# Spectral mixing and a gated feed-forward block on one core: the first batch's loads, buffers and weight roundings rearranged

## The chip, the cores and the metric

One core of a Trainium2 chip. The metric is device time in microseconds (us), the median of several runs. Lower is better. The kernel before took 3157.78 us (median of three runs, 3153.94 to 3158.0).

## The reference, cut to what matters

```python
batch, seq, dim = (8, 3008, 256)            # x: float32
X = np.fft.rfft(x, axis=1)                  # 1505 frequencies
Y = X * (filt_r + 1j * filt_i)[None]        # a learned filter, float32
y = np.fft.irfft(Y, n=3008, axis=1).astype(np.float32)
x = y.reshape(8 * 3008, 256)                # 24064 tokens
g = x @ w_gate                              # 256 -> 1536; the three weights are float64
silu = g * (1.0 / (1.0 + np.exp(-g)))
out = (silu * (x @ w_val) @ w_out).astype(np.float32)
```

The kernel does the transform as matrix products: a first step over 47 rows ("pa"), a middle step per pair of frequencies ("pb", product with the filter, "pc") and an inverse step ("pd"). Between these the data goes through DRAM (d1 and d2) to be regrouped. Then come blocks of the feed-forward part ("hidden blocks", tiles wA, wE, wF with g or v) and its output products (tiles ending in _o), done as seven products for eight. While the hidden blocks of one batch run on TensorE, the transform of the next batch is slipped in between. Only the first batch has nothing to hide behind.

The float64 weights arrive as pairs of 32-bit words and are rounded to float32 by bit operations: 18 "roundings", each a chain over VectorE, ScalarE and GpSimd.

## The kernel before

The parts that the change and the argument touch (`...` marks cuts):

```python
def round_weights(j):
    load_weights(j + 2)                     # two raw buffers, two loads ahead
    ...
    v.tensor_scalar(out=man, in0=high, scalar1=0xFFFFF, scalar2=None, op0=ALU.bitwise_and)
    nc.scalar.activation(out=w, in_=man, func=AF.Copy, scale=2.0 ** -20, bias=1.0)
    v.tensor_scalar(out=pw, in0=high, scalar1=20, scalar2=0x7FF, ...)
    v.tensor_scalar(out=pw, in0=pw, scalar1=-896.0, scalar2=0.0, op0=ALU.add, op1=ALU.max)
    ...                                     # three more operations on VectorE
    nc.gpsimd.tensor_tensor(out=w, in0=w, in1=pw.bitcast(FP32), op=ALU.mult)
    ...                                     # three copies on ScalarE, four sums on GpSimd

def load_tables(self, parts=3):             # first batch: 3 x (1 table + 4 filter parts)
    for i in range(parts):
        nc.sync.dma_start(out=tb[:, ts(i, n)], in_=de_dram[:, ts(i, n)])
        for rows, view in filter_parts():   # 32 partitions each, every second one reversed
            nc.sync.dma_start(out=f[rows, ts(i, n), :], in_=view(n * i, n))
    ...

def stage1(self, u):
    ...
    nc.tensor.matmul(out=ps[0:NK], lhsT=wf_t, rhs=self.x.pop(u), ...)    # pa, 94x96
    nc.scalar.copy(out=t1, in_=ps[0:NK])
    nc.gpsimd.dma_start(out=self.d1_rows[:, ts(u, NV), :], in_=t1)

def stage2a(self, u):
    ...
    ps = fps.tile(...)                      # pb shares two PSUM banks with pa, pc, pd
    ...                                     # two matmuls, four products on VectorE
    add(nc.gpsimd, pt, pt, qt)

def stage2b(self, u):
    ps = fps.tile(...)                      # pc
    ...
    nc.scalar.copy(out=g, in_=ps)
    for p in range(2):
        nc.gpsimd.dma_start(out=self.d2[...], in_=g[64 * p:64 * p + 64])

# the first batch
spec.load_x(0); load_weights(0); load_weights(1); spec.load_tables()
for u in range(N_ONE): spec.stage1(u)
for _ in range(2): round_weights(todo.pop(0))
for u in range(N_TWO + 1):                  # pc follows pb by one step
    if u < N_TWO: spec.stage2a(u)
    if u: spec.stage2b(u - 1)
...
if b == 0 and i == 0:                       # the filter, copied inside DRAM for later batches
    for rows, view in filter_parts():
        nc.scalar.dma_start(out=f_dram[rows], in_=view(0, NS))
```

The order in which each engine runs its instructions is set by a scheduler when the kernel is built. It moves the roundings and the filter copy to where the engine concerned looks free.

## Time and profile before

| Stretch of the kernel before | us from the start |
|---|---|
| first load of d1 (row "t<-d" of SyncE's timeline) | 61.95 |
| first pd | 143.93 |
| first hidden block | 153.92 |
| end of the second output product | 287.07 |
| end of the span | 3160.8 |

The stretches are read from timelines. TensorE's gives each group of matmuls with start, duration, array size and, in square brackets, the idle time before it and what released it.

### The profile page before, as it was taken

What the parts mean: (1) busy time and instruction counts of PE and PEld (TensorE: products, weight loads), DVE (VectorE), ACT (ScalarE), POOL (GpSimd) and SP (SyncE); (2) the same over time, 40 slices, a digit from 0 to 9 for tenths busy, and PEclk for the clock granted to TensorE, in tenths of its full rate; (3) what the DMA queues carried; (4) which work ended last, traced back from release to release, by engine and by line L of the source; (5) the groups of instructions that cost most, each with busy time, mean ns of one, the idle gap of its engine ahead of it and who ended that gap; (6) DMA issues with size and microseconds to landing.
All of it is one profiled execution on the core that took longest, in us unless ns stands there. A gap on an engine that the chain in (4) does not pass through costs nothing.

```text
span 3160.8 us, 40740 instructions
## 1 busy us (share of the span) xinstructions
PE 3059.3 (97%) x15488; PEld 2241.2 (71%) x15488; DVE 1474.2 (47%) x2348; ACT 1150.4 (36%) x2122; POOL 1418.7 (45%) x1662
## 2 busy tenths in 40 slices
PE   4689999999999999999999999999999999999998
PEld 1456777777776777777777677777777677777776
DVE  2664554345544445335543355434554345544443
ACT  1244333333334333333334433333333433333332
POOL 2664454345443445344444445434544345533343
PEclk9589999999999999999999999999999999999999
DMA  8522222213222222122222222221321212210000
GB/s 253 140 87 66 80 67 66 60 54 93 67 57 70 61 73 81 56 62 71 73 64 60 66 77 71 60 67 54 87 74 50 72 55 77 64 30 21 21 8 13
DMA packets 112691, 215.61 MB, mean 68 GB/s; under 512 B 19672, under 2 KB 53464, under 8 KB 111480
## 3 DMA queue, kind: packets, MB, share of 16 engines
q1 hardware_dynamic: 84208, 134.86, 14.9%
q0 software_dynamic: 26624, 75.01, 8.3%
q10 hardware_dynamic: 1664, 3.15, 0.3%
q8 instruction: 122, 2.00, 0.3%
q14 instruction: 73, 0.60, 0.1%
HBM read 137.96 MB, written 78.12 MB: 68 GB/s over the span
## 4 chain that ended last, share of the span: by engine, by line
PE 78%; POOL 7%; DVE 5%; issue 2%; ACT 2%; POOLq 0%; DVEq 0%
PE wA_v L396 15%; PE wA_g L396 15%; PE wA_o L460 7%; PE wE_v L396 7%; PE wE_g L396 7%; PE wE_o L460 7%; PE wF_o L460 4%; PE wF_g L396 4%; PE pd L354 3%; PE wF_v L396 3%; POOL o L160 3%; PE pa L305 3%; POOL h L163 3%; PE pc L336 2%; PE pb L317 2%
## 5 line engine op out<-in xcount | busy, mean ns | idle before, releaser
L396 PE MATMUL wA_v<-y,wv_t 128*128 128x376 f32 x1536 | 614.7, 482 | 10.0 <-ACT u_v L405 9.2
L396 PE MATMUL wA_g<-y,wg_t 128*128 128x376 f32 x1536 | 614.9, 482 | 5.7 <-ACT s L416 3.3
L163 POOL TENSOR_TENSOR h<-h 128x376 f32<-128x376 f32 x576 | 566.7, 984 | 28.8
L160 POOL TENSOR_TENSOR h<-h 128x376 f32<-128x376 f32 x192 | 188.1, 980 | 709.1 <-PE wE_v L396 407.6
L405 ACT COPY u_g<-wA_g 128x376 f32<-128x376 f32 x576 | 269.8, 468 | 588.5 <-PE wA_g L396 585.9
L396 PEld LDWEIGHTS wA_v<-y,wv_t 128*128 128x128 f32 x1536 | 290.1, 190 | 206.6 <-DVE h L418 15.8
L460 PEld LDWEIGHTS wA_o<-wo_t,h 128*128 128x128 f32 x3456 | 406.9, 192 | 16.6 <-issue 0.6
L460 PE MATMUL wA_o<-wo_t,h 128*128 128x128 f32 x3456 | 417.9, 275 | 0.0
L396 PEld LDWEIGHTS wA_g<-y,wg_t 128*128 128x128 f32 x1536 | 281.9, 191 | 173.1 <-issue 28.7
L423 ACT ACTIVATE s<-s 128x1128 f32<-128x1128 f32 x192 | 219.5, 1143 | 375.7 <-DVE s L160 375.7
L425 DVE TENSOR_TENSOR h<-s,h 128x1128 f32<-128x1128 f32 x192 | 258.2, 1345 | 125.6 <-ACT s L423 125.5
L396 PE MATMUL wE_g<-y,wg_t 128*128 128x376 f32 x768 | 308.1, 483 | 0.0
L396 PE MATMUL wE_v<-y,wv_t 128*128 128x376 f32 x768 | 307.6, 482 | 0.2 <-DVE h L160 0.2
L405 ACT COPY u_v<-wA_v 128x376 f32<-128x376 f32 x576 | 272.6, 473 | 69.6 <-PE wA_v L396 65.9
L160 DVE TENSOR_TENSOR s<-u_g,wE_g 128x376 f32<-128x376 f32 x384 | 209.1, 544 | 177.7 <-ACT u_g L405 176.1
L160 DVE TENSOR_TENSOR s<-u_g,wF_g 128x376 f32<-128x376 f32 x192 | 104.5, 544 | 399.2 <-PE wF_g L396 377.8
L460 PE MATMUL wE_o<-wo_t,h 128*128 128x128 f32 x2304 | 281.6, 276 | 7.6 <-DVE o L160 7.6
L460 PE MATMUL wF_o<-wo_t,h 128*128 128x128 f32 x2304 | 278.3, 275 | 0.0
L460 PEld LDWEIGHTS wE_o<-wo_t,h 128*128 128x128 f32 x2304 | 267.5, 192 | 13.7 <-DVE o L160 13.7
L460 PEld LDWEIGHTS wF_o<-wo_t,h 128*128 128x128 f32 x2304 | 267.6, 192 | 0.0
L160 DVE TENSOR_TENSOR h<-u_v,wE_v 128x376 f32<-128x376 f32 x384 | 209.2, 545 | 27.9 <-ACT u_v L405 6.0
L160 POOL TENSOR_TENSOR p<-p,q 128x512 f32<-128x512 f32 x96 | 121.9, 1270 | 212.0 <-DVE q L327 207.3
(66 smaller groups left out, 3285.5 us busy)
## 6 DMA issues: line engine op xcount, KB each, us to landing
d<-t POOLq DMA_DIRECT2D x128, 192.0 KB, 2.4
t<-d SPq DMA_DIRECT2D x192, 128.0 KB, 2.9
d<-g POOLq DMA_DIRECT2D x192, 128.0 KB, 2.6
t<-d SPq DMA_DIRECT2D x64, 384.0 KB, 3.9
tb<-de_tbl SPq DMA_DIRECT2D x84, 256.0 KB, 3.8
f<-filt SPq DMA_DIRECT2D x84, 256.0 KB, 2.7
x<-in_x_dram SPq DMA_DIRECT2D x112, 160.0 KB, 2.3
out_dram<-o POOLq DMA_DIRECT2D x128, 128.0 KB, 2.0
```

The lines of the kernel that those rows point to most:

```text
L160: eng.tensor_tensor(out=dst, in0=a, in1=b, op=ALU.add)
L163: eng.tensor_tensor(out=dst, in0=a, in1=b, op=ALU.subtract)
L305: nc.tensor.matmul(out=ps[0:NK], lhsT=wf_t, rhs=self.x.pop(u), start=True, stop=True)
L317: nc.tensor.matmul(out=ps[:, i, :], lhsT=self.tb[u][:, i, 0, :], rhs=t2[:, i, :], start=True, stop=True)
L336: nc.tensor.matmul(out=ps[:, i, :], lhsT=tb[:, i, 1, :], rhs=pt[:, i, :], start=True, stop=True)
L354: nc.tensor.matmul(out=psv[:, n, :], lhsT=self.t4[k, i][:, n, ts(cb, 128)], rhs=wi_t, start=True, stop=True)
L396: nc.tensor.matmul(out=bk[z][kind], lhsT=wt[z][:, j, LEFT[p], :], rhs=y[:, RIGHT[p], :], start=start, stop=True, skip_group_check=True)
L405: nc.scalar.copy(out=u[(1, 6, 7).index(p)], in_=bk[z]["A"])
L423: nc.scalar.activation(out=s[:, 0:3], in_=s[:, 0:3], func=AF.Silu)
L425: nc.vector.tensor_tensor(out=h[:, 0:3], in0=s[:, 0:3], in1=h[:, 0:3], op=ALU.mult)
L460: nc.tensor.matmul(out=bk[kind][:, t, :], lhsT=hs[i][:, HID[p], t0:t0 + 128], rhs=wo_t[:, JB * q + i, RIGHT[p], :], start=start and t == 0 ...
```

## The change

The intent: make the first batch shorter. The pb of the first batch get six PSUM banks of their own, and pc follows by three steps instead of one. The table loads go to ScalarE's queue and half of the d2 writes to ScalarE. Roundings are held in program order ("pin") so that they cannot slide into the first batch. One of their operations goes to ScalarE, and three copies vanish because GpSimd writes straight to the destination. The filter is no longer copied inside DRAM. The diff, cut to its core:

```diff
-    f_dram = fdpool.tile([128, NS, C], FP32, name="filt")
+        pin = tc.keep_in_program_order
-        v.tensor_scalar(out=man, ...)
-        nc.scalar.activation(out=w, in_=man, func=AF.Copy, ...)
-        v.tensor_scalar(out=pw, in0=pw, scalar1=-896.0, scalar2=0.0, op0=ALU.add, op1=ALU.max)
+        pin(v.tensor_scalar(out=man, ...))
+        pin(nc.scalar.activation(out=w, in_=man, func=AF.Copy, ...))
+        pin(nc.scalar.activation(out=pw, in_=pw, func=AF.Relu, bias=off_t))
-        nc.gpsimd.tensor_tensor(out=w, in0=w, in1=pw.bitcast(FP32), op=ALU.mult)
+        pin(e.tensor_tensor(out=dst[:, 0:4, :]..., in0=w, in1=pw.bitcast(FP32), op=ALU.mult))
-            for p, a in ((1, w[:, 0, 0]), (2, w[:, 0, 1]), (4, w[:, 1, 1])):
-                nc.scalar.copy(out=dst[:, LEFT[p]], in_=a)
...                                     # load_x: into the space of weights not yet there
-                    nc.sync.dma_start(out=self.f[u], in_=f_dram[:, ss])
+                    for rows, view in filter_parts():
+                        self.load(out=self.f[u][rows], in_=view(NV * u, NV))
-                nc.sync.dma_start(out=tb[:, ts(i, n)], in_=de_dram[:, ts(i, n)])
+                nc.scalar.dma_start(out=tb[:, ts(i, n)], in_=de_dram[:, ts(i, n)])
                 for rows, view in filter_parts():
-                    nc.sync.dma_start(out=f[rows, ts(i, n), :], in_=view(n * i, n))
+                    nc.scalar.dma_start(out=f[rows, ts(i, n), :], in_=view(n * i, n))
-            nc.gpsimd.dma_start(out=self.d1_rows[:, ts(u, NV), :], in_=t1)
+            queue = nc.scalar if self.b == 1 else nc.gpsimd
+            queue.dma_start(out=self.d1_rows[:, ts(u, NV), :], in_=t1)
+                ps = bank("AEF"[u % 3], f"b_{u}").rearrange("p (i c) -> p i c", i=NV)
-                nc.gpsimd.dma_start(out=self.d2[...], in_=g[64 * p:64 * p + 64])
+                queue = nc.scalar if self.b == 0 and p else nc.gpsimd
+                queue.dma_start(out=self.d2[...], in_=g[64 * p:64 * p + 64])
-        spec.load_x(0)
+        for i in range(4):
+            spec.load_x(i)
+        spec.load_tables()
         load_weights(0)
         load_weights(1)
-        spec.load_tables()
-        for u in range(N_TWO + 1):
+        lag = 3
+        for u in range(N_TWO + lag):
-            if b == 0 and i == 0:
-                for rows, view in filter_parts():
-                    nc.scalar.dma_start(out=f_dram[rows], in_=view(0, NS))
```

More of the change, by code (lines that the diff above doesn't have):

```diff
@@ L62 @@
 N_TWO = NS // NV
-LEFT = {1: 0, 2: 1, 4: 2, 5: 3, 6: 4, 7: 5, 3: 6}
+LEFT = {1: 0, 2: 1, 7: 2, 4: 3, 5: 4, 6: 5, 3: 6}
 RIGHT = {1: 0, 2: 1, 3: 2, 4: 3, 5: 4, 6: 5, 7: 6}
+WO = {1: 0, 7: 1, 2: 2, 3: 3, 5: 4, 6: 5, 4: 6}
 HID = {1: 0, 6: 1, 4: 2, 2: 3, 5: 4, 7: 5, 3: 6}
@@ L134 @@
     dpool = pool("dram", 2, DRAM)
-    fdpool = pool("fdram", 1, DRAM)
     fps = pool("fps", 2, PSUM)
@@ L143 @@
     wo_t = cpool.tile([128, NJ, 7, 128], FP32)
-    f_dram = fdpool.tile([128, NS, C], FP32, name="filt")
+    off_t = cpool.tile([128, 1], FP32)
+    nc.vector.memset(off_t, -896.0)
     def filter_parts():
@@ L205, in round_weights @@
         flat2 = "p a b f two -> p (a b f) two"
-        v.tensor_scalar(out=man, in0=high, scalar1=0xFFFFF, scalar2=None, op0=ALU.bitwise_and)
-        nc.scalar.activation(out=w, in_=man, func=AF.Copy, scale=2.0 ** -20, bias=1.0)
-        v.tensor_scalar(out=pw, in0=high, scalar1=20, scalar2=0x7FF,
-                        op0=ALU.logical_shift_right, op1=ALU.bitwise_and)
-        v.tensor_scalar(out=pw, in0=pw, scalar1=-896.0, scalar2=0.0, op0=ALU.add, op1=ALU.max)
+        pin = tc.keep_in_program_order
+        pin(v.tensor_scalar(out=man, in0=high, scalar1=0xFFFFF, scalar2=None,
+                            op0=ALU.bitwise_and))
+        pin(nc.scalar.activation(out=w, in_=man, func=AF.Copy, scale=2.0 ** -20, bias=1.0))
+        pin(v.tensor_scalar(out=pw, in0=high, scalar1=20, scalar2=0x7FF,
+                            op0=ALU.logical_shift_right, op1=ALU.bitwise_and))
+        pin(nc.scalar.activation(out=pw, in_=pw, func=AF.Relu, bias=off_t))
         v.tensor_scalar(out=pw, in0=pw, scalar1=255.0, scalar2=2.0 ** 23,
@@ L218, in round_weights, with bank @@
                                op0=ALU.mult, op1=ALU.add)
-        nc.gpsimd.tensor_tensor(out=w, in0=w, in1=pw.bitcast(FP32), op=ALU.mult)
         e = nc.gpsimd
+        pin(e.tensor_tensor(out=dst[:, 0:4, :].rearrange("p (a b) f -> p a b f", b=2), in0=w,
+                            in1=pw.bitcast(FP32), op=ALU.mult))
         if left:
-            for p, a in ((1, w[:, 0, 0]), (2, w[:, 0, 1]), (4, w[:, 1, 1])):
-                nc.scalar.copy(out=dst[:, LEFT[p]], in_=a)
-            add(e, dst[:, LEFT[5]], w[:, 1, 0], w[:, 1, 1])
-            sub(e, dst[:, LEFT[6]], dst[:, LEFT[5]], w[:, 0, 0])
-            sub(e, dst[:, LEFT[7]], w[:, 0, 0], w[:, 1, 0])
-            sub(e, dst[:, LEFT[3]], w[:, 0, 1], dst[:, LEFT[6]])
-        else:
-            for p, a in ((1, w[:, 0, 0]), (2, w[:, 1, 0]), (3, w[:, 1, 1])):
-                nc.scalar.copy(out=dst[:, RIGHT[p]], in_=a)
-            sub(e, dst[:, RIGHT[5]], w[:, 0, 1], w[:, 0, 0])
-            sub(e, dst[:, RIGHT[6]], w[:, 1, 1], dst[:, RIGHT[5]])
-            sub(e, dst[:, RIGHT[7]], w[:, 1, 1], w[:, 0, 1])
-            sub(e, dst[:, RIGHT[4]], w[:, 1, 0], dst[:, RIGHT[6]])
+            a11, a12, a21, a22, s1, s2, s4 = [dst[:, i] for i in range(7)]
+            add(e, s1, a21, a22)
+            sub(e, s2, s1, a11)
+            sub(e, a21, a11, a21)
+            sub(e, s4, a12, s2)
+        else:
+            b11, b12, b21, b22, t1, t2, t4 = [dst[:, i] for i in range(7)]
+            sub(e, t1, b12, b11)
+            sub(e, t2, b22, t1)
+            sub(e, b12, b22, b12)
+            sub(e, t4, b21, t2)
+    def bank(kind, name):
+        return wps.tile([128, 512], FP32, name=f"w{kind}_{name}", tag=kind)
     class Spectral:
@@ L247, in __init__, with load @@
             self.x, self.t2, self.f, self.tb, self.p, self.t4, self.y = {}, {}, {}, {}, {}, {}, {}
+        def load(self, **kw):
+            ins = nc.sync.dma_start(**kw)
+            if self.b == 1:
+                tc.keep_in_program_order(ins)
         def load_x(self, u):
             if self.b == 0:
-                if u == 0:
-                    rows = x[0].rearrange("(r n) c -> r n c", n=32)
-                    for i in range(4):
-                        xt = spool0.tile([NR, 8, C], FP32, name=f"x0_{i}", tag="x", bufs=2)
-                        for r in (slice(0, 80), slice(80, NR)):
-                            nc.sync.dma_start(out=xt[r], in_=rows[r, ts(i, 8), :])
-                        for j in range(8 // NV):
-                            self.x[8 // NV * i + j] = xt[:, ts(j, NV), :]
+                rows = x[0].rearrange("(r n) c -> r n c", n=32)
+                for a, n in ((0, NV), (NV, 8 - NV)) if u == 0 else ((0, 8),):
+                    for r in (slice(0, 80), slice(80, NR)):
+                        nc.sync.dma_start(out=x0[u][r, a:a + n, :],
+                                          in_=rows[r, 8 * u + a:8 * u + a + n, :])
+                for j in range(8 // NV):
+                    self.x[8 // NV * u + j] = x0[u][:, ts(j, NV), :]
             elif u < N_ONE:
@@ L263, in load_x @@
                 for r in (slice(0, 80), slice(80, NR)):
-                    nc.sync.dma_start(out=self.x[u][r], in_=rows[r, ts(u, NV), :])
+                    self.load(out=self.x[u][r], in_=rows[r, ts(u, NV), :])
         def load_two(self, u):
@@ L268, in load_two @@
                 b = self.b
-                ss = ts(u, NV)
                 if b:
                     self.tb[u] = tbpool.tile([128, NV, 2, 128], FP32, name=f"tb_{b}_{u}", tag="tb")
-                    nc.sync.dma_start(out=self.tb[u], in_=de_dram[:, ss])
+                    self.load(out=self.tb[u], in_=de_dram[:, ts(u, NV)])
                     self.f[u] = fpool.tile([128, NV, C], FP32, name=f"f_{b}_{u}", tag="f")
-                    nc.sync.dma_start(out=self.f[u], in_=f_dram[:, ss])
-                self.t2[u] = t2pool.tile([128, NV, C], FP32, name=f"t2_{b}_{u}", tag="t2")
+                    for rows, view in filter_parts():
+                        self.load(out=self.f[u][rows], in_=view(NV * u, NV))
+                p2 = spool0 if b == 0 and u % 2 else t2pool
+                self.t2[u] = p2.tile([128, NV, C], FP32, name=f"t2_{b}_{u}", tag="t2", bufs=2)
                 for p in range(2):
@@ L306, in stage1 @@
             nc.scalar.copy(out=t1, in_=ps[0:NK])
-            nc.gpsimd.dma_start(out=self.d1_rows[:, ts(u, NV), :], in_=t1)
+            queue = nc.scalar if self.b == 1 else nc.gpsimd
+            queue.dma_start(out=self.d1_rows[:, ts(u, NV), :], in_=t1)
         def stage2a(self, u):
-            if u == 0:
-                self.load_two(0)
-            self.load_two(u + 1)
+            ahead = 3 if self.b == 0 else 1
+            for v in range(ahead) if u == 0 else ():
+                self.load_two(v)
+            self.load_two(u + ahead)
             t2, f = self.t2.pop(u), self.f.pop(u)
-            ps = fps.tile([128, NV, C], FP32, name=f"pb_{self.b}_{u}", tag="f")
+            if self.b:
+                ps = fps.tile([128, NV, C], FP32, name=f"pb_{self.b}_{u}", tag="f")
+                ppool, qpool = apool, bpool
+            else:
+                ps = bank("AEF"[u % 3], f"b_{u}").rearrange("p (i c) -> p i c", i=NV)
+                ppool = apool if u % 3 == 2 else spool0
+                qpool = bpool if u % 2 else spool0
             for i in range(NV):
@@ L318, in stage2a @@
                                  start=True, stop=True)
-            pt = apool.tile([128, NV, C], FP32, name=f"p_{self.b}_{u}", tag="p")
-            qt = bpool.tile([128, NV, C], FP32, name=f"q_{self.b}_{u}", tag="q")
+            pt = ppool.tile([128, NV, C], FP32, name=f"p_{self.b}_{u}", tag="p",
+                            bufs=4 if ppool is spool0 else 2)
+            qt = qpool.tile([128, NV, C], FP32, name=f"q_{self.b}_{u}", tag="q", bufs=1)
             lo, hi = slice(0, 64), slice(64, 128)
@@ L337, in stage2b @@
                                  start=True, stop=True)
-            g = gpool.tile([128, NV, C], FP32, name=f"g_{self.b}_{u}", tag="g")
+            p3 = spool0 if self.b == 0 and u % 2 else gpool
+            g = p3.tile([128, NV, C], FP32, name=f"g_{self.b}_{u}", tag="g", bufs=2)
             nc.scalar.copy(out=g, in_=ps)
@@ L341, in stage2b @@
                 a0 = p * NS + NV * u
-                nc.gpsimd.dma_start(out=self.d2[a0:a0 + NV].rearrange("s n c -> n s c"),
-                                    in_=g[64 * p:64 * p + 64])
+                queue = nc.scalar if self.b == 0 and p else nc.gpsimd
+                queue.dma_start(out=self.d2[a0:a0 + NV].rearrange("s n c -> n s c"),
+                                in_=g[64 * p:64 * p + 64])
         def stage3(self, k, step):
@@ L374, in stage3 @@
                 sub(nc.gpsimd, block(4), block(2), block(6))
-    def bank(kind, name):
-        return wps.tile([128, 512], FP32, name=f"w{kind}_{name}", tag=kind)
     hids, outs = {}, {}
@@ L460, in product @@
                     nc.tensor.matmul(out=bk[kind][:, t, :], lhsT=hs[i][:, HID[p], t0:t0 + 128],
-                                     rhs=wo_t[:, JB * q + i, RIGHT[p], :],
+                                     rhs=wo_t[:, JB * q + i, WO[p], :],
                                      start=start and t == 0 and i == 0, stop=True,
@@ L500 @@
     nc.sync.dma_start(out=wf_t, in_=wf_dram.ap())
+    wo_f = wo_t.rearrange("p j i f -> p (j i f)")
+    x0 = [wo_f[0:NR, 0:8 * C], wo_f[0:NR, 8 * C:16 * C]]
+    x0 += [t[0:NR, NJ // 2:].rearrange("p j i f -> p (j i f)")[:, 0:8 * C] for t in (wg_t, wv_t)]
+    x0 = [t.rearrange("p (n c) -> p n c", c=C) for t in x0]
     spec = Spectral(0)
     with tc.tile_pool(name="start", bufs=1) as spool0:
-        spec.load_x(0)
+        for i in range(4):
+            spec.load_x(i)
+        spec.load_tables()
         load_weights(0)
         load_weights(1)
-        spec.load_tables()
         nc.sync.dma_start(out=wi_t, in_=wi_dram.ap())
@@ L511 @@
             round_weights(todo.pop(0))
-        for u in range(N_TWO + 1):
+        lag = 3
+        for u in range(N_TWO + lag):
             if u < N_TWO:
                 spec.stage2a(u)
-            if u:
-                spec.stage2b(u - 1)
+            if u >= lag:
+                spec.stage2b(u - lag)
     for i in range(2):
```

## The prediction

> **What bounds the kernel now.** I read the page's busy shares and slices first, then the stretches by window, then the timelines of each engine for the first 240 us, then the waits there.
>
> The page says TensorE is the bound, and its slices say where it is not:
>
> ```profile
> PE 3059.3 (97%) x15488; PEld 2241.2 (71%) x15488; DVE 1474.2 (47%) x2348; ACT 1150.4 (36%) x2122; POOL 1418.7 (45%) x1662
> ...
> PE   4689999999999999999999999999999999999998
> ...
> DMA  8522222213222222122222222221321212210000
> ```
>
> From the third slice (237 us) on TensorE is full; only the first 225 us have room. The change touches nothing later except how the filter is loaded. The stretches by window (start:end, length, busy us and count of PE, PEld, DVE, ACT, POOL, clock, DMA share, GB/s) split these 225 us into four:
>
> ```profile
> 0.00:62.00 62.00, 28.79 (x32) 7.88 (x32) 6.40 (x12) 13.07 (x25) 15.54 (x30) 1.00 1.01 286
> 62.00:144.00 82.00, 48.27 (x97) 27.98 (x97) 54.13 (x86) 14.28 (x36) 47.17 (x64) 0.64 0.50 140
> 144.00:154.00 10.00, 7.23 (x33) 6.99 (x34) 4.46 (x10) 3.36 (x7) 4.87 (x9) 0.50 0.39 110
> 154.00:226.00 72.00, 56.89 (x156) 30.94 (x156) 54.72 (x84) 32.85 (x79) 49.68 (x65) 0.86 0.33 104
> 226.00:320.00 94.00, 93.78 (x483) 68.02 (x483) 38.97 (x62) 36.56 (x67) 39.11 (x48) 1.00 0.20 60
> ```
>
> Row 1: loads, first step (pa) and its write to DRAM; DMA is full. Row 2: the middle steps (pb, product, pc); nothing is full. Row 3: the inverse step (pd). Row 4: four hidden blocks while weights are still being rounded. Row 5 is the steady state. The waits of TensorE in row 2:
>
> ```profile
> PE pc L336 <- POOL p L160: 13.9, 8, 5.7
> PE pb L317 <- DMA t<-d: 10.7, 1, 10.7
> PE pd L354 <- DMA t<-d: 8.4, 1, 8.4
> PE pb L317 <- ACT g L339: 7.0, 10, 0.7
> ```
>
> pb and pc share two PSUM banks, so pb waits for the copy of g that empties the bank, and pc waits for GpSimd. The timeline shows one step of it:
>
> ```profile
> 91.13 2.08 PE L336 MATMUL pc<-p,tb 128*128 128x256 f32 x4
> 93.88 2.07 PE L317 MATMUL pb<-t,tb 128*128 128x256 f32 x4 [0.68 <-ACT g L339]
> 96.65 2.07 PE L336 MATMUL pc<-p,tb 128*128 128x256 f32 x4 [0.70 <-POOL p L160]
> ```
>
> Two steps take 10.6 us, 5.3 each. The same four matmuls took 1.13 us once, at 82.95 us: otherwise TensorE ran here at half clock.
>
> **What the Trainium skill says.** (1) "TensorE: Matmul & The Clock Gate", Part 1, the HAM clock gate: half clock by default, full after about 3.4 us of sustained work, half again after an idle window. The trace agrees for 128x128 matmuls (full clock at about 81.5 us after nearly gapless work; half again after 2.2 us of idling at 201 us) but not for pa: 10.5 us without a gap from 11.36 us stayed slow, 1.76 us a step, against 1.02 us for one pa later. I take pa on its 94x96 array to stay slow. (2) The same page, on the array and engine queue depths: ScalarE, VectorE and GpSimd queues are strict first in, first out. The trace agrees: at 145.9 us the copy of y was ready but stood behind a weight copy that waited for GpSimd, and ran at 149.53. (3) "DMA: Bandwidth & Descriptors", "Issuing engines are not separate DMA queues": another issuer saves issue time, not bandwidth. The first 62 us moved 286 GB/s at a share of 1.01 with three issuers at work, so a fourth route adds nothing. (4) "SBUF — State Buffer", "Who interferes with whom": VectorE in a two-port mode and GpSimd exclude each other. The rounding's tensor_scalar took 1.20 us at 177.57, beside a GpSimd add, against 0.43 alone.
>
> **The change, part by part.**
>
> *A. Loads (row 1, first t load now at 61.95 us).* Removed: the 3.15 MB copy of the filter inside DRAM. x then has less to share with. But the tables (6.3 MB, 15 DMAs) move to ScalarE's queue, ahead of all its copies, and the built program has eight DMA semaphores in rotation over both queues: ScalarE's fifth table load waits for an x load, its tenth for the last big x load, its fifteenth for the third weight load. So ScalarE cannot copy the first pa before x, some 5.5 MB of tables and 0.75 MB of weights have landed: 3.08 + 5.5 + 0.75 = 9.3 MB at 286 GB/s is 32.6 us, less a little for what is still in flight, so about 30 us; then a table load of 1.28. From there 16 pa run at 1.77 us: 31.5 + 0.6 + 0.6 + 14 x 1.77 = 57.5 us, then 0.6 for the copy or issue and some 2.5 to landing (median 2.4): the first t load at 61 us. Gain 1 us: DMA stops being the bound and the slow pa row after a late ScalarE takes its place.
>
> *B. Middle steps (82 us now, to the first pd).* pb gets six banks, so it no longer waits for g; pc has two of its own; four t buffers instead of two; half of the d2 writes leave GpSimd's queue (0.61 us each); the rounding instructions that sat in between (five roundings, 3.1 us of VectorE and 3.4 of GpSimd each) are gone. Floors per step: VectorE 4 x 0.69 = 2.8; GpSimd 1.27 + 0.61 = 1.9; TensorE 2.3 at full clock, 4.15 at half. But GpSimd is in order, and in the built order each write of g stands before a later add, so its round trip counts: add 1.3, pc 1.15 (full clock), copy and semaphores 0.9, issue 0.65 = 4.0 us. In the built order four steps stand alone (4.0 each) and eight in pairs (a pair is 4.0 + 1.27 + 0.63 = 5.9): 4 x 4.0 + 4 x 5.9 = 39.6 us, 3.3 a step. Ahead of it: t load 4.05 (as at 61.95 to 66.00), pb 2.1, VectorE 2.8 = 9, and 2.8 because pc 0 stands behind five pb. Behind it: landing 2.6 and t4 load 4.1. Sum 9 + 2.8 + 39.6 + 6.7 = 58. Gain 82 - 58.5 = 23.5.
>
> *C. pd (10 us now).* The copies of y no longer stand behind weight copies: 2.77 us of wait falls. Gain 2.5.
>
> *D. Hidden blocks beside roundings.* Before, nine of 18 roundings remained at 154 us; in the 72 us of row 4 TensorE did 4 x 14 x 0.635 + 8 x 0.88 + 1.9 = 44.5 us of full-clock work: 27 us lost. Now 14 roundings remain and spread over six hidden blocks. VectorE: each rounding falls from 3.1 to 2.7 (one operation goes to ScalarE as a Relu, and three weight copies vanish there); two roundings with the lock of (4) were 9.4 us at 174.48 to 189.1, so now 7.8; 7 x 7.8 + 6 x 6.2 (seven short operations at 0.54 and one of 2.45) + 4 for pd and output sums = 96 us, and at 93% of it busy 103. TensorE's work in that time: 6 x 8.9 + 14.1 (first output) + 12 pa and 8 pd, 12 = 79. Lost 24. Gain 3. Holding roundings back therefore moves work from a stretch where it delayed B to one where it nearly fills VectorE; it is not removed.
>
> *E. After that.* The filter loads of the seven later batches become four DMAs instead of one, 84 loads, on a queue that is idle mostly, at a DMA share of 0.2. Order on TensorE is unchanged there apart from the first blocks. Gain 0.
>
> Sum: 1 + 23.5 + 2.5 + 3 + 0 = 30; 3157.8 - 30 = 3128 us.
>
> **The rivals.**
> 1. *ScalarE is not blocked, or pa reaches full clock.* If the copies begin at 15 us, or pa takes 0.95 us, d1 is complete at 48 us instead of 61: gain 43, 3115 us. Against it: the waits in the built program and the four rows of slow pa. For it: one pa row without gaps of 25 us was not seen before.
> 2. *TensorE stays at half clock in the middle.* Its 63 to 80% share is near what did not suffice between 89 and 131 us. Each of eight round trips grows by 0.95: 7.6 us less gain, 3136 us.
> 3. *The held-back roundings cost more than row 4 shows.* Each new block of weights waits on an in-order chain over VectorE, ScalarE and GpSimd, and ScalarE now also issues the next batch's d1 writes, each with a semaphore wait. At 8.5 us a rounding, 14 take 119 us, lost 40: gain 14, 3144 us.
> 4. *Everything works:* 1 and D at half its loss together give 55, 3103 us.
>
> **Range and chances.** Nothing outside the first 240 us can pay, and of these some 180 are loss (225 less 44.5 of work); over 2% is 63 us, a third of it, more than rival 4. Rivals 2 and 3 together leave some 6. So 3102 to 3150 for 8 in 10; faster by over 2%: 0.06; within 2%: 0.92; slower: 0.02.
>
> **What would show it.** A: ScalarE's first copy of pa at about 31 us, its queue filled with table loads before; pa at 1.77 us. B: first t load to first pd 58 us, pb no longer waiting for g, GpSimd waiting for g. C: pd rows 7.5 us. D: from pd to the last rounding about 103 us. E: 226 us onwards as long as before per block. I am wrong if the copies of pa begin before 20 us, if pb and pc take 2.08 us throughout B, if TensorE waits more than 40 us in D, or if waits for filter loads appear in later batches.

## More of the kernel before

From the second output product on, TensorE is busy without a break. So a change at the start is worth what it moves the end of that product. Two rows of the stretches by window cover the hidden blocks up to it (start:end, length, busy us and count of TensorE, weight loads, VectorE, ScalarE, GpSimd, granted clock, DMA share, GB/s; the granted clock is the share of full speed that the profile records for TensorE):

```profile
153.92:239.03 85.11, 70.00 (x272) 44.05 (x272) 57.80 (x88) 35.36 (x82) 54.80 (x71) 0.88 0.28 88
239.03:287.07 48.04, 47.82 (x240) 33.82 (x239) 18.99 (x30) 18.74 (x34) 21.52 (x26) 1.00 0.22 66
```

TensorE needs 117.8 of these 133.2 us. The other lines of the profile are in the prediction.

## The result and the profile after

The changed kernel took 3151.53 us (median of four runs, 3149.37 to 3152.5), the kernel before 3157.6 (four runs of the same rounds, 3153.94 to 3158.0). A ratio is the mean time of one kernel's fast runs over that of the other's of the same rounds, so not quite the ratio of the medians. Here it is 0.9982, with a 95% interval of 0.9965 to 1.0: the same within 2%. The result is correct. The gain is 6 us where 30 were predicted, and 3151.53 lies just outside the predicted range.

The page of the changed kernel, TensorE's share and the slices:

```profile
PE 3042.9 (97%) x15488; PEld 2236.8 (71%) x15488; DVE 1461.6 (46%) x2331; ACT 1149.9 (37%) x2086; POOL 1409.8 (45%) x1634
...
PE   3689999999999999999999999999999999999999
...
DMA  8432322213222223122222222221321212210000
```

TensorE's first slice fell from 4 tenths to 3: there is less work in the first 79 us, not more. The second and third, 6 and 8, are as before. DMA has 4 tenths in the second slice instead of 5 and 3 instead of 2 in the third: loads have moved later. The stretches by window, cut at the same events as in the prediction (first load of d1, first pd, first hidden block, ends of the first two output products):

```profile
0.00:73.00 73.00, 28.51 (x32) 8.18 (x32) 2.55 (x6) 11.62 (x19) 9.68 (x21) 1.00 0.81 187
73.00:133.20 60.20, 30.78 (x97) 21.99 (x97) 35.61 (x53) 8.34 (x14) 27.56 (x34) 0.78 0.49 135
133.20:140.10 6.90, 6.90 (x33) 6.90 (x33) 1.41 (x2) 1.64 (x2) 0.43 (x1) 0.50 0.12 18
140.10:225.00 84.90, 69.24 (x272) 43.05 (x272) 56.39 (x91) 39.72 (x69) 62.65 (x73) 0.89 0.39 118
225.00:278.00 53.00, 50.09 (x239) 34.14 (x238) 33.21 (x55) 23.84 (x44) 37.95 (x45) 0.97 0.34 103
```

Row 1 has grown from 62 to 73 us, row 2 has shrunk from 82 to 60.2, row 3 from 10 to 6.9. Rows 4 and 5 together last 138 us, where the kernel before needs 133. A program that gives back in two places what it gains in two others explains the small sum. To know how far single profiles can be trusted, the kernel before was profiled three times in all and the changed one twice (see the last experiments). The means:

| Stretch | before (3 profiles) | after (2 profiles) | difference | predicted |
|---|---|---|---|---|
| A: start to first load of d1 | 60.7 | 71.9 | +11.3 | -1 |
| B: to first pd | 81.7 | 60.1 | -21.6 | -23.5 |
| C: to first hidden block | 10.0 | 6.9 | -3.1 | -2.5 |
| D: to end of second output product | 133.4 | 139.2 | +5.8 | -3 |
| E: to the end | 2873.8 | 2871.8 | -2.0 | 0 |
| sum | 3159.4 | 3150.0 | -9.5 | -30 |

B and C came as predicted; A and D went the other way.

**What holds A.** ScalarE's timeline of the changed kernel (ACTq is its sequencer issuing a DMA; a wait before such a row lies inside the row's duration or ahead of it):

```profile
21.56 13.43 ACTq L303 DMA_DIRECT2D f<-in_filt_i_dram  x2
...
40.66 1.28 ACT L320 ACT_TABLE_LOAD   x1 [40.66 <-DMA raw<-in_moe_w_val_dram]
41.95 1.07 ACT L320 COPY t<-pa 96x512 f32<-96x512 f32 x2
44.64 0.58 ACT L320 COPY t<-pa 96x512 f32<-96x512 f32 x1 [1.63 <-PE pa L319]
```

ScalarE copies nothing before 41.95 us. Its queue holds 15 table loads. Each may be issued only when a DMA semaphore (the counter by which a finished transfer is reported) of a rotation of eight is free again; the prediction read this rotation in the built program, while the trace shows the waits alone. Two loads issued in the row at 21.56 kept ScalarE for 13.43 us. By the releaser that the profile names, the last wait ended with a weight load on SyncE's queue, which shares the rotation. From there the copies come every 1.7 us, at the pace of pa, but for one wait of 3.87 us on a write of d1.

**What holds D.** ScalarE around 206 us, then TensorE:

```profile
206.36 0.63 ACT L212 ACTIVATE w<-w 128x512 f32<-128x512 uint32 x1 [3.90 <-DVE w L210]
206.95 0.72 ACT L215 ACTIVATE pw<-pw,off_t 128x512 uint32<-128x512 uint32 x1
...
207.58 0.45 ACT L428 COPY u_v<-wA_v 128x376 f32<-128x376 f32 x1
```

```profile
208.08 0.90 PE L419 MATMUL wA_v<-y,wv_t 128*128 128x376 f32 x2 [3.88 <-ACT u_v L428]
```

The rounding's activation at 206.36 stood first in ScalarE's queue and waited 3.90 us for VectorE. Behind it stood the copy of u_v, which empties a PSUM bank. TensorE waited 3.88 us for that copy. VectorE in its turn had waited for GpSimd:

```profile
205.90 0.43 DVE L210 TENSOR_SCALAR w<-raw 128x512 uint32<-128x512 uint32 x1 [3.30 <-POOL wg_t L226]
```

L226 is the product of the rounding before, which reads `w`; there is one buffer of `w`, and the next rounding begins by writing it. VectorE waits 19 us in D for these products, and GpSimd is busy 100.8 of its 138 us, against 76.3 before. In D TensorE waits 18.6 us in all, against 15.3 before (lengths of the two rows less TensorE's busy time), and runs longer for the same matmuls, 119.6 us against 117.8. By releaser, 6.5 of the 18.6 us are waits for u_v, 5.6 for h and s from VectorE and 4.5 for a load of x. The chain above is thus seen in single waits; it is not shown to make up the whole.

### The profile page after: what moved, and what is told of

Same layout as the page of the kernel before. It is cut to its first block, busy times and chain, and to the rows that moved or that the text cites. A ratio compares the mean times of both kernels' runs of the same rounds, so it can differ in the third digit from the quotient of the medians.

```text
span 3150.0 us, 41042 instructions
## 1 busy us (share of the span) xinstructions
PE 3042.9 (97%) x15488; PEld 2236.8 (71%) x15488; DVE 1461.6 (46%) x2331; ACT 1149.9 (37%) x2086; POOL 1409.8 (45%) x1634
## 4 chain that ended last, share of the span: by engine, by line
PE 80%; POOL 8%; DVE 5%; issue 3%; DMA 2%; ACT 2%; SPq 0%; POOLq 0%; ACTq 0%; DVEq 0%
PE wA_v L419 15%; PE wA_g L419 15%; PE wA_o L483 7%; PE wE_v L419 7%; PE wE_g L419 7%; PE wE_o L483 7%; PE wF_o L483 4%; PE wF_g L419 4%; PE pd L380 4%; PE wF_v L419 3%; PE pa L319 3%; POOL o L162 3%; POOL h L165 3%; PE pc L360 3%; PE pb L340 2%
## 5 line engine op out<-in xcount | busy, mean ns | idle before, releaser
L419 PEld LDWEIGHTS wE_v<-y,wv_t 128*128 128x128 f32 x768 | 146.3, 191 | 102.1 <-DVE h L162 5.1
```

The source lines that it names most:

```text
L419: nc.tensor.matmul(out=bk[z][kind], lhsT=wt[z][:, j, LEFT[p], :], rhs=y[:, RIGHT[p], :], start=start, stop=True, skip_group_check=True)
```

## The experiments

All times below are medians of the fast runs of an experiment, with the kernel before in the same rounds at 3156.85 to 3157.32 us. The changed kernel of the result has 3151.5.

### 1. The table loads on SyncE's queue (e1_tables_sync)

Theory for A: ScalarE stands behind its own DMA issues. Rival: the loads need that long whoever issues them.

```diff
-                nc.scalar.dma_start(out=tb[:, ts(i, n)], in_=de_dram[:, ts(i, n)])
+                nc.sync.dma_start(out=tb[:, ts(i, n)], in_=de_dram[:, ts(i, n)])
                 for rows, view in filter_parts():
-                    nc.scalar.dma_start(out=f[rows, ts(i, n), :], in_=view(n * i, n))
+                    nc.sync.dma_start(out=f[rows, ts(i, n), :], in_=view(n * i, n))
```

> The changed kernel with the 15 table loads back on SyncE's queue, behind the x loads. Theory (ScalarE cannot copy the first pa before it has issued its own table loads, each held by a semaphore of another load): the first copy of pa moves from 42 us to about 13, the pa run at 1.7 us from there or wait for x, and the first t load, which now stands behind all tables in SyncE's queue, moves from 73 us to about 50 (13.5 MB at 286 GB/s and 2 us of start); the time falls by some 23, to 3128. Rival (the bytes have to arrive at the rate seen, 223 GB/s, whoever issues them): the copies begin early but the first t load comes at 62 or later, and the time falls by 10 at most, to 3141.

Measured: 3131.03 us (3127.74 to 3133.44), ratio to before 0.9918 (0.9904 to 0.9933). ScalarE's timeline:

```profile
6.51 0.58 ACT L320 COPY t<-pa 96x512 f32<-96x512 f32 x1 [4.48 <-PE pa L319]
```

The first copy comes at 6.51 us instead of 41.95, the first load of d1 at 50.58 instead of 72.97. B, C and D stay within 2.2 us of the changed kernel. Of 22 us gained in A, 20 reach the end. The theory holds: the choice of the queue that issues the loads costs 20 us here, because ScalarE's queue also has work to do.

### 2. The same loads in fewer and wider pieces (e2_f_wide, e5_f_wide4)

Both give a wrong result: the filter tile is filled from wrong places, with the same bytes. e2 reads each third of each filter tile with one load of 128 partitions, so six table loads instead of 15. e5 keeps 15 loads, but each filter load spans 128 partitions with rows of 2 KB.

```diff
-                for rows, view in filter_parts():
-                    nc.scalar.dma_start(out=f[rows, ts(i, n), :], in_=view(n * i, n))
+                for j in range(4):                                   # e5; e2: one load
+                    nc.scalar.dma_start(out=f[:, n * i + 2 * j:n * i + 2 * j + 2, :],
+                        in_=bass.AP(..., ap=[[11 * C, 128], [C, 2], [1, C]]))
```

> Wrong result on purpose: the changed kernel, but each third of the filter for the first batch is one load of 128 partitions with 8 KB rows (of the wrong rows) instead of four loads of 32 partitions, half of them in rows of 1 KB; the bytes are the same. Theory (the four narrow, short-rowed loads are why the loads ran at 223 GB/s and not at the 286 I reckoned with): ScalarE's first copy moves from 42 us to about 34, the first t load from 73 to 65, and the time falls by 8, to 3143. Rival (the rate is low for another reason, or the rotation of eight semaphores paces it): ScalarE's first copy stays at 39 to 42 us and the time within 2 us.

> Wrong result on purpose, to part what the run with one wide load a third had mixed: the filter's thirds are again four loads each, 15 table loads on ScalarE's queue as in the changed kernel, but each of 128 partitions with rows of 2 KB (of the wrong rows). If the shape of the loads set the rate (206 to 222 GB/s from 10 to 30 us, 280 with wide loads): the rate is about 270 again and ScalarE's first copy at about 34 us, the first t load at 66, the time 3144. If the number of ScalarE's loads in the rotation of semaphores set it: the first copy stays at 40 us or so. A first copy at 18, as with six loads, would say that the count does not matter and the shape is all.

Measured: e2 3133.68 us (3133.1 to 3137.45), first copy at 17.6 us; e5 3135.22 (3134.35 to 3136.86), first copy at 24.92, first load of d1 at 57.08. Both gained about twice what was expected. Stretches by window between 10 and 41 us, the changed kernel first, then e5:

```profile
10.00:20.00 10.00, 3.98 (x4) 0.79 (x4) 0.00 (x0) 0.00 (x0) 0.00 (x0) 1.00 1.06 206
20.00:30.00 10.00, 0.00 (x0) 0.00 (x0) 0.00 (x0) 0.00 (x0) 0.00 (x0) 1.00 1.04 222
30.00:41.00 11.00, 0.00 (x0) 0.00 (x0) 0.76 (x2) 0.34 (x1) 0.00 (x0) 1.00 1.06 235
```

```profile
10.00:20.00 10.00, 3.98 (x4) 0.79 (x4) 0.00 (x0) 0.00 (x0) 0.00 (x0) 1.00 1.02 260
20.00:30.00 10.00, 4.44 (x6) 1.55 (x7) 0.00 (x0) 3.51 (x5) 1.72 (x3) 1.00 1.04 309
30.00:41.00 11.00, 8.16 (x11) 2.50 (x10) 0.34 (x1) 2.33 (x4) 2.56 (x5) 1.00 1.03 326
```

With the same count of loads and bytes, the rate rises from 206 to 235 GB/s up to 260 to 326 GB/s. (In e5's last two rows writes of d1 take part.) The first window, without such writes in either kernel, has 260 against 206. So the shape of the filter loads is why the prediction's 286 GB/s did not come: in the kernel before, that rate was a mix with other transfers. Experiment 1 agrees. With its narrow loads unchanged it moved 9.10 MB from 10 to 41 us, of which GpSimd's writes of d1 were 2.32; the other 6.77 MB make 218 GB/s, where the changed kernel moved 6.86 MB, or 221, and nothing beside them. One difference of e2 and e5 is not parted from the shape: they read the same rows of the filter for every third. With six loads, of 8 KB rows, ScalarE is free 7 us sooner than with e5's 15 of 2 KB; which of the two does it was not tested, and the times of e2 and e5 overlap.

### 3. Rows or partitions (e11_f_long)

The filter loads differ from e5's in two ways: they span 32 partitions, and every second one has reversed order, so rows of 1 KB. Here the reversed ones are read forwards (wrong result), so all are 32 partitions with rows of 8 KB.

```diff
-                off, step = (0, 1) if half == 0 else (N1, -1)
+                off, step = (0, 1) if half == 0 or flat else (N1, -1)   # flat: in load_tables only
```

> Wrong result on purpose: as the changed kernel, but the reversed half of each first filter load is read forwards, so all twelve are 32 partitions with rows of 8 KB, none with rows of 1 KB. If the 1 KB rows make the loads slow: 260-330 GB/s between 10 and 41 us, first copy of pa at 24-30 us, time 3134-3142 us. If the 32 partitions do: 205-240 GB/s, first copy at 39-42 us, time 3149-3153 us.

Measured: 3150.68 us (3148.41 to 3151.18). Rates in the three windows 217, 228 and 265 GB/s, first copy at 39.59 us, where two profiles of the changed kernel have 41.95 and 39.74 (the second of them has 207, 225 and 264 GB/s). Long rows are worth little. What is left is the span of 32 partitions, save for the repeated rows named above. The Trainium skill has this, and the prediction missed it: "SBUF — State Buffer", section "Door 1: The DMA port swizzle (why `[64,N]` ≈ `[32,N]`)", says that partitions 0 to 31 reach half of the ports and gives 189 GB/s at 1 MiB for them against 328 for all 128. The 206 to 235 GB/s of the changed kernel, a mix of both kinds, agree.

### 4. pa on a padded array (e8_pa_128)

The first batch's pa is padded with zeros from 94x96 to 128x128: the table by its host constant, x by a memset of partitions 64 to 127 ahead of its loads. Nothing is asked of TensorE but larger matmuls with the same moving rows.

```diff
-    wf_t = cpool.tile([NR, NK], FP32)
+    wf_t = cpool.tile([128, 128], FP32)
-            nc.tensor.matmul(out=ps[0:NK], lhsT=wf_t, rhs=self.x.pop(u), ...)
+            if self.b == 0:
+                nc.tensor.matmul(out=ps, lhsT=wf_t, rhs=self.x.pop(u), ...)
```

> The changed kernel with the first batch's pa padded with zeros from 94x96 to 128x128; each takes as many columns through TensorE as before. If the size of the array in use decides whether its clock rises: pa falls from 1.7 to about 0.9 us after some 4 us, the 16 pa end some 12 us earlier, the first t load at 61 instead of 73 us and the time by 12, to 3139. If zeros or these steps do not count, or the clock is held for another reason: pa stays at 1.7 us and the time within 2 us of 3151.

Measured: 3140.24 us (3138.46 to 3140.76), ratio 0.9945 (0.993 to 0.996). TensorE's timeline, a row of the changed kernel, then one of e8:

```profile
54.95 7.04 PE L319 MATMUL pa<-wg_t,wf_t 94*96 94x512 f32 x8
```

```profile
48.95 3.76 PE L320 MATMUL pa<-wg_t,wf_t 128*128 128x512 f32 x8
```

Each row is four pa without a gap. In the changed kernel pa ran gapless from 51.43 to 68.8 us and stayed at 1.7 us. In e8 it falls to 0.9 us a pa from 47 us on, after 6.5 us at the slow rate and a gap of 1.6. So here the smaller array in use kept pa slow, and zeros in the rest were enough to speed it up. That this is TensorE's clock is read from the durations (a 94x96 pa among the hidden blocks takes 1.02 us, at 172.16 us): the profile's granted clock reads 1.00 from the start in both kernels, for pa of 1.76 us and of 0.94 us alike. Whether the rows or the columns of the array count was not parted. The first load of d1 comes at 60.63 us instead of 72.97 and the time falls by 11.

### 5. Roundings not held back (e3_unpinned)

Theory for D: holding the roundings in order costs. Rival: the roundings of the changed kernel are dear in themselves (the Relu on ScalarE, the sums in place).

```diff
-        pin = tc.keep_in_program_order
+        pin = lambda ins: ins
```

> The changed kernel with the roundings free to be scheduled earlier again (only the next batch's loads stay pinned). Four more roundings then stand in the first step and three at the end of the middle steps, as the built order shows. Theory (the held-back roundings cost the stretch from the first hidden block to the end of the second output product its 5 us more, because VectorE, ScalarE and GpSimd wait for one another in order there): that stretch falls from 138 us to 128 or less, the middle steps grow by 3 at most, and the time falls by 5 to 8, to 3145. Rival (holding them back pays, as intended): the first or the middle steps grow by more than the stretch falls, and the time is 3152 or more.

Measured: 3136.62 us (3134.55 to 3139.11), ratio 0.9938 (0.9921 to 0.9955). The stretches of D by window, to be set beside the last two rows of the changed kernel:

```profile
139.79:214.17 74.38, 65.83 (x272) 42.27 (x272) 49.98 (x79) 35.48 (x63) 55.06 (x63) 0.91 0.33 102
214.17:262.21 48.04, 47.82 (x240) 33.83 (x239) 18.83 (x30) 18.65 (x34) 18.57 (x20) 1.00 0.26 77
```

D is 122.4 us instead of 138.1, A and B within half a us. The same matmuls take 113.7 us of TensorE instead of 119.6, and the waits are 8.8 us instead of 18.6: 5.9 and 9.8 make the 15.7. The reason is in ScalarE's timeline: without the order, ten roundings run before the first hidden block: four during A, two where B begins, four from the last pc to the first hidden block. Eight are left for D, as in the kernel before. With the order, two run before and 16 fall into D. The rival falls: with eight roundings in D in both, this D takes 122.4 us where the kernel before needs 133.4. What part of the change makes these 11 us was not tested. The change that was to keep roundings out of B's way left B as it was (60.4 against 60.2 us) and filled D.

### 6. Who issues the next batch's d1 writes (e4_d1_pool)

Rival for D: ScalarE's new duty of issuing the second batch's d1 writes.

```diff
-            queue = nc.scalar if self.b == 1 else nc.gpsimd
+            queue = nc.gpsimd
```

> The changed kernel with the second batch's d1 writes issued by GpSimd again, not by ScalarE. Theory (the rounding chain is what makes the hidden stretch long): the stretch of 138 us changes by less than 2 us, the time stays within 2 of 3151. Rival (ScalarE, held at its 16 new DMA issues, delays the copies that TensorE waits for): the stretch falls by 4 or more and the time to 3147 or less.

Measured: 3152.31 us (3151.57 to 3154.99); D 137.6 us instead of 138.1. This rival falls.

### 7. Both repairs together (e6_sync_unpinned)

The edits of 1 and 5 in one kernel.

> The changed kernel with both repairs: tables on SyncE's queue and the roundings unpinned. Theory (two separate losses, the late first copy and the roundings crowded beside the hidden blocks): first t load at about 51 us as with the first repair alone, the stretch from the first hidden block to the end of the second output product below 133 us, the time 3123 or less; adding both gains in full (20 and 15) would give 3116, but the weights now arrive behind the tables, so fewer roundings fit into the first step. Rival (both repairs free the same time): 3130.

Measured: 3128.4 us (3126.06 to 3128.95). The gains do not add: 15 us from the roundings alone, but 2.6 on top of experiment 1. With the tables ahead of them in SyncE's queue, the weights arrive late, and only two roundings run before the middle steps, as when held back. D is 134.9 us.

### 8. Both halves of each g written by ScalarE (e7_g_act)

B's theory in the prediction was a round trip through GpSimd, 4.0 us for a step alone and 5.9 for a pair. GpSimd's timeline of the changed kernel:

```profile
88.26 0.65 POOL L368 DMA_DIRECT2D d<-g  x1 [2.10 <-ACT g L364]
88.92 2.50 POOL L162 TENSOR_TENSOR p<-p,q 128x512 f32<-128x512 f32 x2
92.30 0.63 POOL L368 DMA_DIRECT2D d<-g  x1 [0.88 <-ACT g L364]
94.03 0.59 POOL L368 DMA_DIRECT2D d<-g  x1 [1.10 <-ACT g L364]
...
98.02 0.60 POOL L368 DMA_DIRECT2D d<-g  x1 [2.10 <-ACT g L364]
```

From the write at 88.26 to the one at 94.03 a pair of steps takes 5.77 us; the next step stands alone and takes 3.99, to 98.02. Each write waits for the copy of g that the adds before it made possible. The experiment takes the write out of GpSimd's queue, on top of e6:

```diff
-                queue = nc.scalar if self.b == 0 and p else nc.gpsimd
+                queue = nc.scalar if self.b == 0 else nc.gpsimd
```

> As the run before, and ScalarE issues both d2 writes of each middle step, so that GpSimd's adds no longer stand behind the wait for a copy of g. Theory (in the middle steps GpSimd's in-order round trip of 4 us a group sets the pace, as the prediction had it): the step falls to VectorE's 2.8 us, first t load to first pd falls from 60 to about 51 us, the time by 9 against the run before. Rival (DMA landing or TensorE at half clock paces the steps): that part stays above 57 us.

Measured: 3118.92 us (3117.17 to 3120.82), ratio 0.9876 (0.986 to 0.9893). ScalarE's timeline:

```profile
74.96 0.59 ACT L364 COPY g<-pc 128x512 f32<-128x512 f32 x1 [2.24 <-PE pc L360]
75.58 1.24 ACTq L368 DMA_DIRECT2D d<-g  x2
77.78 0.59 ACT L364 COPY g<-pc 128x512 f32<-128x512 f32 x1 [2.24 <-PE pc L360]
```

A step now takes 2.82 us (74.96 to 77.78), the prediction's floor of VectorE. B falls from 61.9 to 54.4 us and the time by 9.5. The expectation was 51 us for B. The round trip is shown.

### 9. All findings in one kernel (e9_best)

e7, with the padding of 4 and with the first two weight loads ahead of the tables.

```diff
-        spec.load_tables()
         load_weights(0)
         load_weights(1)
+        spec.load_tables()
```

> All findings together: the first two weight loads ahead of the tables, the tables on SyncE's queue, roundings not held back, both halves of every g write on ScalarE, pa on a zero-padded 128x128 array. Theory: holding back is dear only when the weights have arrived early, so the hidden stretch falls from 135.5 us (the earlier run with all but the weight order and the padding) to 120-126 us; the first t load stays near 50 us because loads and the d1 write share the DMA there; the middle steps take 52-55 us; time 3100-3110 us. Rival: the weight order is worth nothing once roundings are free, hidden stretch 133-136 us, time 3115-3120 us.

Measured: 3113.33 us (3112.36 to 3114.99), ratio to before 0.9861 (0.9846 to 0.9876), correct. First load of d1 at 52.03 us, B 53.6, D 126.8. A is no shorter than in e7 (50.93 us): with the weight loads ahead of the tables, the padding shows no gain there. D falls by 8.7 us against e7. Four roundings now run before the first product with the filter instead of two, and eleven fall into D instead of twelve, so part of this gain is not explained by the count. The time is 3 us above the expected range. This is the fastest kernel, 38 us ahead of the changed one. Its interval overlaps that of e7, from other rounds, so the step from e7 to it is not sure in size.

### 10. The rest of the tables behind the first loads of d1 (e12_best_defer)

```diff
-        spec.load_tables()
+        spec.load_tables([0])
...
+            if u == 0 and self.b == 0:
+                self.load_tables([1, 2])     # after the first three loads of d1
```

> As the run with all findings together, with the second and third part of the tables loaded behind the first three t loads, where the DMA has room. Theory: 4.2 MB less before the first t load at about 290 GB/s, so the first t load comes 10-14 us sooner, at 36-41 us; the middle steps grow by 0-4 us; time 3090-3102 us. Rival: the middle steps wait for the late tables and give the gain back, 3100-3110 us.

Measured: 3120.64 us (3118.93 to 3124.19), a miss. The first load of d1 comes at 42.45 us, 9.6 sooner, but B grows from 53.6 to 68.2. SyncE's timeline:

```profile
49.42 7.48 SPq L305 DMA_DIRECT2D f<-in_filt_i_dram  x2
56.94 0.45 SPq L303 DMA_DIRECT2D tb<-de_tbl  x1
57.43 6.52 SPq L305 DMA_DIRECT2D f<-in_filt_r_dram  x2
64.00 0.91 SPq L305 DMA_DIRECT2D f<-in_filt_i_dram  x2
64.96 1.23 SPq L292 DMA_DIRECT2D t<-d  x2
```

The issues of the deferred loads stand in one queue with the loads of d1 for the following steps, each waiting for its semaphore. The fourth step's pb waited 9.93 us for its load. It is the fault of experiment 1 again, on another engine.

### 11. The filter copy alone (e10_before_nocopy, r4_nocopy)

The kernel before with one part of the change.

```diff
-                    nc.sync.dma_start(out=self.f[u], in_=f_dram[:, ss])
+                    for rows, view in filter_parts():
+                        nc.sync.dma_start(out=self.f[u][rows], in_=view(NV * u, NV))
...
-                for rows, view in filter_parts():
-                    nc.scalar.dma_start(out=f_dram[rows], in_=view(0, NS))
```

> The kernel before with one part of the change: the filter is never copied inside DRAM; later batches load it from the input in four parts. Theory (the first stretch of the kernel before is bound by DMA volume): 3.15 MB read and written less at about 286 GB/s gives a first t load at 50-55 us instead of 62, everything after it as before, time 3146-3151 us, and no waits for filter loads in later batches. Rival (slow pa and its copies bound the stretch): first t load at 60-62 us, time 3155-3158 us. Second rival: 84 loads instead of 21 cost later: time above 3158 us.

> The kernel before without the filter copy, profiled again. If its gain of 9 us at the first t load is real: 52-54 us again, and the missing gain must be lost in the middle steps or the hidden stretch (the four timed runs were 2.8 us slower than the profiled one). If it scatters: first t load at 55-62 us.

Measured: 3157.83 us (3155.04 to 3158.51), ratio 1.0002 (0.9985 to 1.0019). In two profiles the first load of d1 came at 53.05 and 54.51 us, where the kernel before has 59.6 to 62, and the second output product ended at 279.6 and 280.1 instead of 283.2 to 287.1. So the two profiles show some 6 us of gain and four runs show none, with an interval that allows 4.7. Later loads of the filter never hold TensorE: after that product it waited for nothing but sums of o (7.3 us in all). Whether the part is worth 0 or 5 us stays open.

### 12. The scatter of the profiles (r1_before, r2_before, r3_after)

The unchanged kernels once more, one look each (single runs, so of unknown state; their clocks, 0.985, 0.985 and 0.991, are those of the first profiles).

> The kernel before, unchanged, profiled again. If its first profile was typical: first t load 60-63 us, hidden blocks begin at 152-155 us, second output product ends at 285-289 us. If it was a slow one: one of the stretches is 4-8 us shorter, and the end of the second output product comes at 279-283 us; then the predicted terms were missed by that much less or more than the first comparison said.

> As the run ahead of it, a third profile of the kernel before: the stretch that differs in one of the two profiles is the one that scatters. Expected where nothing scatters: all stretches within 1 us of the first profile.

> The changed kernel, profiled again. Expected: first t load 72-74 us, middle steps 59-61 us, hidden blocks to the second output product 137-139 us, since five experiments that left these parts alone showed them within 2 us. A stretch outside these says that the changed kernel scatters as well.

Measured: the kernel before 3158.92 and 3162.49 us, the changed one 3151.72. Before, A was 59.56 and 60.44 us, D 133.1 and 133.9; after, A 70.90 and D 140.2. So both losses keep sign and size in every pairing. The profiled runs of the kernel before (3158.92 to 3162.7) lie above most of its timed ones, which is why the profiles show 9.5 us of gain and the timed runs 6. Why that is was not found.

## Why the prediction was right or wrong

**A was wrong, by 12 us, in one term.** That ScalarE would stand behind its loads was right, and it is shown (experiment 1). So was the volume: 9.0 MB by 41 us (the sum of rate times length over the windows to there), where 9.3 were expected. The term that failed is the rate. It was taken from the kernel before, 286 GB/s, where the filter copy and the writes of d1 ran beside the table loads. With those gone and ScalarE blocked, the loads ran alone, at 9.0 MB / 41 us = 220 GB/s, held by their span of 32 partitions (experiments 2 and 3). The first copy thus came at 41.95 and 39.74 us instead of 31.5. The 16 slow pa after it took about as long as said: 27 us from first copy to last, for 26.

**B was right:** -21.6 us against -23.5, by the mechanism named: TensorE waits for GpSimd, GpSimd for g, in steps of 3.99 us alone and 5.77 a pair. Experiment 8 removes it and B falls. (In the sum for B the parts make 58.1 us, and 58.5 was taken off.)

**C was right:** -3.1 against -2.5.

**D was wrong, by 9 us.** The failed step is "14 roundings remain ... lost 24". It took D as a sum of VectorE's work. VectorE was busy 89.6 of 138 us, so it was not full. Sixteen roundings fell there, not 14 (and eight in the kernel before, not nine, by the activations in ScalarE's timeline), and the waits were 18.6 us; with eight roundings there they are 8.8 (experiment 5). How a rounding costs TensorE time is seen in single waits: its first operation on VectorE waits for GpSimd's product of the rounding before, its activation at the head of ScalarE's queue waits for VectorE, and a copy that TensorE needs waits behind it, after which TensorE runs slowly for a time. A second buffer of `w`, which would part this chain from the amount of work, was not tried. The text did say that held-back roundings move work rather than remove it. It did not see that the free order had placed most of them where they cost nothing: beside A and in the wait of pd for its data (experiment 5).

**E was right:** the 9 us between the two kernels at the second output product are, in the first profiles, there after the last (8.9 and 9.1), and no waits for filter loads appeared. The 2 us of the table lie behind the last product and were not looked into.

**The rivals.** The first (ScalarE free, or pa fast) did not happen, but experiments 1 and 4 made its two halves, 20 and 11 us. The second (half clock in B) came in part: from 108 us on the granted clock was 0.50, and steps there took 4.95 us where 3.99 was the pace before, some 3 us over three steps (the first three pb were slow too). B's 60.1 us are 2 more than the 58 foretold. The third (held-back roundings cost more) happened, by another mechanism than the one that sized it, the next batch's d1 writes on ScalarE being no part of it (experiment 6); its 3144 us came without the loss in A. The range failed because no rival let A grow.

## What to carry to other kernels

An engine that issues DMAs runs its computing work behind them, so ask for each issue what it waits for and what stands behind it: the same loads cost 20 us more on a queue with copies in it than on SyncE's, and cost again on SyncE as soon as urgent loads stood there. A rate read from a stretch belongs to the mix of transfers in it; when the change removes part of the mix, work out the rate of what is left from its shape. Before holding work back, look at where the free order had put it: here it lay in waits, and the order moved it to the stretch where it cost 15 us.

## What the Trainium skill lacked or had wrong

- "DMA: Bandwidth & Descriptors", section "Issuing engines are not separate DMA queues", says that another issuing engine saves only issue time. For bandwidth this agrees: between 10 and 41 us the loads moved at 221 GB/s with the tables on ScalarE's queue and at 218 with them on SyncE's (experiments 1 and 2). The section lacks that the issuer's own work waits behind issues that wait for semaphores: the move from ScalarE to SyncE was worth 22 us in A and 20 in time (experiment 1), and 7.48 and 6.52 us in single rows of SyncE (experiment 10).
- "TensorE: Matmul & The Clock Gate", Part 1, ties the clock to sustained activity and names a window of about 3.4 us. It lacks that the part of the array in use counts: 94x96 matmuls without a gap for 17 us stayed at 1.7 us a pa, the same padded with zeros to 128x128 came down to 0.9 us. Its idle window has the same length; in the kernel before, the granted clock fell to 0.50 after 2.24 us of idling (at 201 us), which the prediction's point (1) counts as agreement though it is less than the window.
- No page that was read for this says what a rotation of few DMA semaphores over several queues costs: by the profile's releaser, ScalarE waited until a weight load on SyncE had landed, at 40.66 us.
